# 64-bit weights of an attention and two feed-forward blocks: the conversion to 32 bits done in the loaded tile by a rescale, a shift, the sign and an integer addition

## The chip, the cores and the metric

The kernel runs on one core of a Trainium2 chip. The metric is the time of one execution on the device in microseconds (us). The core's engines run side by side and wait for one another by semaphores: TensorE (PE, with PEld for its weight loads), VectorE (DVE), ScalarE (ACT), GpSimd (POOL) and SyncE (SP), whose queue issues all the loads and stores here.

## What is computed

Three blocks follow one another. The attention block takes `x` (8 batches, 8 heads, 512 rows of 64) and `state` (8, 8, 32 rows of 64): the rows of x read the state by a softmax over 32, and the state reads x by a softmax over 512. Its output, 544 rows per batch, is 4352 rows of 512. Then come

```
h = maximum(x @ w_in, 0)            # w_in  512 x 2048
x = (h * h) @ w_out                 # w_out 2048 x 512
y = (((x @ w1) * (x @ w2)) @ w3) @ w_out2   # 512 x 1024 twice, 1024 x 1024, 1024 x 512
```

The inputs are arrays of 32-bit and 64-bit floats: x and state come as 32-bit, all six weight matrices as 64-bit floats. The output is 32-bit, 4352 x 512.

## The kernel before

**Matmuls in three passes.** An operand is split into a high part, rounded to the matmul's own 32-bit type, and a low part, the remainder (`split`, L80 to L85: the high part a copy, mostly on ScalarE, the low part a subtraction on VectorE). A product is three matmuls, high x high, low x high and high x low.

**First stage (up to about 640 us).** An outer loop goes over tiles (c, f), c a batch (or 8, for the state's rows of all batches), f one of 16 blocks of 128 columns of `w_in`. `h_tile` (L448) makes the hidden block, which ScalarE relus and squares and ScalarE and VectorE split (`ghl`); `y_tile` (L483), two tiles behind, multiplies it by the row block f of `w_out` into four accumulators (L494). `make_sw` (L421, matmuls at L426) makes state x `w_in` for a batch and 512 columns. For the first batches the attention steps (`att_steps`) run between the tiles. The first tiles need the converted blocks of `w_in` and `w_out` soon: `win0` in two halves of columns, each of two tiles, before and beside the first tiles; then `w_out` 0 to 7 and so on.

**Conversions.** All weights arrive as 64-bit words. One conversion handles 128 x 512 words: `load64` (L112) loads them into a raw tile of 128 x 512 x 2 32-bit words, low word first, so that the low and the high words are each every second word of the tile. `exponents` (L126) cuts the exponent bits out of the high words on VectorE (L128) and rescales them to the 32-bit exponent on ScalarE (L129, a relu with a bias tile). `convert64` (L132) then runs four operations on VectorE: the mantissa's upper bits as an integer (L146), plus the low words scaled by 2^-32 (L149), the sign bit into the exponent (L152), and mantissa times exponent into the target (L155). There are 72: four for `win0`, 12 for the rest of `w_in` and 16 for `w_out`, and 40 for the weights of the second block (`later`), which are stored to scratch in memory as 32-bit. A converted `w_out` block goes through the tile `cw` and is split (`make_wout`, L186).

**What sets the order.** `convs` (L568) lists the conversions; `conv` (L581) runs the next one, makes the exponents of the one after it ahead, and issues the load three further (`load_next`). Jobs hang on the tiles of the first stage by `side` and `late`, one `conv` per tile at first, from tile 32 on one for every second tile. Raw tiles come from a pool of three buffers (tag `raw`, L110), which loads of x share; the first few raw tiles lie in buffers of `w_out`. The exponents have two buffers (tag `ce`), the mantissa one (`cm`). The order written out is not the order on the engines: a planner orders each engine's instructions by its own estimate of when they can start, and gives the waits; `issue_after` ties a job to an instruction on its engine. On the chip each engine then works through its list in order.

**Later stages.** From about 640 us the second block's weights, all converted by then, are read back, multiplied together (L707) and used in `quad` (L822), `ab9` (L877) and `out_tile` (L903). Nothing of the change runs there but through the time at which it starts.

Of the kernel before, what the change touches and what calls it, by code (L numbers as in the profile page):

```python
# [8 lines left out]
F32 = mybir.dt.float32  # L9
F32R = mybir.dt.float32r  # L10
I32 = mybir.dt.int32
U32 = mybir.dt.uint32
ACTF = mybir.ActivationFunctionType
ALU = mybir.AluOpType
# [6 lines left out]
def kernel(  # L21
# [17 lines left out]
    nc = tc.nc  # L39
# [6 lines left out]
    P = 128  # L46
# [8 lines left out]
    scale = 1.0 / float(D) ** 0.5  # L55
# [3 lines left out]
    def f32(ap):  # L59
        return ap.bitcast(F32)  # L60

    const = ctx.enter_context(tc.tile_pool(name="const", bufs=1))
# [3 lines left out]

    ident = const.tile([P, P], F32, name="ident")
    make_identity(nc, ident)
    ebias = const.tile([P, 1], F32, name="ebias")
    nc.vector.memset(ebias, -896.0 * 2.0**23)  # L70
    def bank_m(name):
        return psum.tile([P, 512], F32, tag="m", bufs=2, name=name)

# [26 lines left out]
    att = att_cm.__enter__()  # L100
# [3 lines left out]
    raws = {}  # L104
# [16 lines left out]
            nc.sync.dma_start(flat, src.bitcast(I32))  # L121
        raws[key] = t

    exps = {}

    def exponents(key, t):  # L126
        e = att.tile([P, 512], I32, tag="ce", bufs=2, name="ce")
        nc.vector.tensor_single_scalar(e, t[:, :, 1], 0x7FF00000, op=ALU.bitwise_and)  # L128
        nc.scalar.activation(e, e, ACTF.Relu, bias=ebias, scale=8.0)  # L129
        exps[key] = e  # L130

    def convert64(key, out):  # L132


        t = raws.pop(key)
        hw, lw = t[:, :, 1], t[:, :, 0].bitcast(U32)
        if len(out.shape) == 3:
            n = out.shape[2]
            hw, lw = (v.rearrange("p (k n) -> p k n", n=n) for v in (hw, lw))
        if key not in exps:  # L140
            exponents(key, t)
        e = exps.pop(key)
        m = att.tile([P, 512], I32, tag="cm", bufs=1, name="cm")
        if len(out.shape) == 3:
            e, m = (v.rearrange("p (k n) -> p k n", n=n) for v in (e, m))
        nc.vector.tensor_scalar(  # L146
            out=m, in0=hw, scalar1=0xFFFFF, scalar2=0x100000, op0=ALU.bitwise_and, op1=ALU.bitwise_or
        )
        nc.vector.scalar_tensor_tensor(  # L149
            out=f32(m), in0=lw, scalar=2.0**-32, in1=m, op0=ALU.mult, op1=ALU.add  # L150
        )
        nc.vector.scalar_tensor_tensor(  # L152
            out=e, in0=hw, scalar=-(2**31), in1=e, op0=ALU.bitwise_and, op1=ALU.bitwise_or
        )
        nc.vector.scalar_tensor_tensor(  # L155
            out=out, in0=f32(m), scalar=2.0**-20, in1=f32(e), op0=ALU.mult, op1=ALU.mult
        )

    def load_win(fg, k):
        load64(("win", fg, k), w_in[k * P:(k + 1) * P, fg * 512:(fg + 1) * 512])  # L160
# [1 line left out]
    def make_win(fg, k):  # L162
        if k == 0:
            win_t[fg] = wpool.tile([P, ND, 512], F32, tag=f"wi{fg // 2}", bufs=2, name=f"win{fg}")
        convert64(("win", fg, k), win_t[fg][:, k, :])
# [6 lines left out]
    def make_win0(half, kk):  # L172
        if win_t[0] is None:
            win_t[0] = wpool.tile([P, ND, 512], F32, tag="wi0", bufs=2, name="win0")
        convert64(("win0", half, kk), win_t[0][:, 2 * kk:2 * kk + 2, half * 256:(half + 1) * 256])
# [6 lines left out]
    def close_splits():  # L182
        while open_splits:
            open_splits.pop(0)()

    def make_wout(f):  # L186
        w = att.tile([P, 512], F32, tag="cw", bufs=1, name="cw")
        convert64(("wo", f), w)

        def halves():  # L190
            t = wpool.tile([P, 2, DM], F32R, tag="wo", bufs=NF, name=f"wo{f}")
            split(t[:, HI], t[:, LO], w)
            wo_t[f] = t

        open_splits.append(halves)
# [330 lines left out]
        nc.scalar.copy(stT[:, 4 * half:4 * half + 4].rearrange("p b k n -> p (b k n)"), ps)  # L526

    warm = const.tile([P, 1], F32, name="warm")
    nc.scalar.activation(warm, ebias, ACTF.Exp, scale=0.0)
    for g in range(G):  # L530
        load_x(0, g, True)
    load_win0(0, 0, True)
# [42 lines left out]
    def load_next():  # L575
        k = convs[pos[0]] if pos[0] < len(convs) else None
        pos[0] += 1
        if k:
            {"wo": load_wout, "win": load_win, "later": load_later}[k[0]](*k[1:])

    def conv():  # L581


        close_splits()
        k, k1 = (convs[i] if i < len(convs) else None for i in (pos[1], pos[1] + 1))
        pos[1] += 1
        if k and k not in exps:
            exponents(k, raws[k])
        if k1:
            exponents(k1, raws[k1])  # L590
        if k:
            {"wo": make_wout, "win": make_win, "later": make_later}[k[0]](*k[1:])
            load_next()
# [6 lines left out]
    side[0] = [lambda: make_win0(1, 0), lambda: make_win0(1, 1), s2[0]]  # L600
    side[1] = [*xp1, lambda: make_sw(0, 0, slice(256, 512)), lambda: make_wout(0), a2t[0], s2[1], sc1]
    side[2] = [conv, s1a1[0], a2t[1], s1b1[0], at1[0]]
    side[3] = [conv, s21[0], sr, s1a1[1], srt, a2t1[0], conv, s1b1[1], sw(1, 0), at1[1]]
    side[4] = [conv, s21[1], lambda: make_st(1)]
    side[5] = [conv, a2t1[1]]
    side[6] = [conv, conv, sr1]
# [401 lines left out]
```

## Time and profile before

| what | value |
| --- | --- |
| time, median of 3 runs | 1257.79 us (1257.4 to 1259.08) |
| profiled execution | 1257.84 us, its span 1256.1 us |
| TensorE busy | 1235.1 us, 98% of the span |
| VectorE busy | 789.0 us, 63% |
| ScalarE busy | 659.3 us, 52% |
| TensorE's granted clock, mean | 0.999 |

The span goes from the first instruction to the last. Busy times of the engines overlap. The profile is of one execution; a line of it names the line of the code, the engine, the operation, and the tiles written and read. TensorE's granted clock is the share of full speed: 1.0 is 2.4 GHz, and a stretch with a value between 0.5 and 1.0 had a part at 1.2 GHz.

### The profile page before, as it was taken

The numbers are of one execution on the slowest core, as the hardware profiler recorded it, in microseconds if no ns is written. First come the engines' busy times: TensorE is split into PE (matmuls) and PEld (weight loads), VectorE is DVE, ScalarE is ACT, GpSimd is POOL, SyncE is SP. The second block draws the span as 40 slices with busy tenths as digits, with TensorE's granted clock in tenths as the row PEclk, the third lists the DMA queues.
The fourth block names the chain that finished last, engine by engine and source line by source line (L and its number), as shares of the span: only waits on it lengthen the run. The fifth ranks groups of instructions, "written<-read, shape, count | busy, mean of one in ns | idle before, by whom it ended". The sixth has DMA issues, their size and how long they took to land.

```text
span 1256.1 us, 17499 instructions
## 1 busy us (share of the span) xinstructions
PE 1235.1 (98%) x6672; PEld 982.1 (78%) x6672; DVE 789.0 (63%) x1403; ACT 659.3 (52%) x1188; POOL 33.5 (3%) x30
## 2 busy tenths in 40 slices
PE   6999999999999999999999999999999999999998
PEld 4667777777777777777799888888888888887886
DVE  6998778677585867742435835555655647474753
ACT  5687768666575756645655434444443524242430
POOL 0000000000000000000000000001500010000000
PEclk9999999999999999999999999999999999999999
DMA  6264646462634535201313520313430521423213
GB/s 218 69 207 145 173 129 201 113 184 82 156 130 86 190 76 173 89 18 34 134 42 111 201 76 9 120 48 126 143 134 9 201 76 52 149 74 128 76 59 117
DMA packets 125268, 143.23 MB, mean 114 GB/s; under 512 B 71680, under 2 KB 75264, under 8 KB 124672
## 3 DMA queue, kind: packets, MB, share of 16 engines
q1 hardware_dynamic: 125184, 142.11, 36.5%
q8 instruction: 52, 0.85, 0.3%
q14 instruction: 32, 0.26, 0.1%
HBM read 96.47 MB, written 45.61 MB: 113 GB/s over the span
## 4 chain that ended last, share of the span: by engine, by line
PE 93%; DMA 2%; ACT 2%; DVE 2%; issue 1%; SPq 0%; ACTq 0%; DVEq 0%
PE y L494 29%; PE po L903 14%; PE qa L822 10%; PE qd L822 7%; PE qc L822 3%; PE ps_w L707 3%; PE qe L822 3%; PE ps_sw L426 3%; PE ab L877 2%; DMA x<-in_x_dram 1%; PE ps_w L692 1%; PE ps_a L364 1%; PE ps_r L372 0%; PE ps_s L295 0%; DMA out_dram<-o 0%
## 5 line engine op out<-in xcount | busy, mean ns | idle before, releaser
L494 PE MATMUL y<-ghl,wo 128*128 128x512 f32 (+1 forms) x1728 | 403.0, 381 | 0.6 <-ACT wo L84 0.5
L494 PEld LDWEIGHTS y<-ghl,wo 128*128 128x128 f32 x1728 | 309.1, 188 | 88.4 <-ACT r L442 12.6
L85 DVE TENSOR_TENSOR ghl<-r,ghl 128x512 fp32r<-128x512 f32 (+1 forms) x144 | 95.0, 660 | 170.1 <-ACT ghl L84 167.4
L822 PE MATMUL qa<-yq,wq 128*128 128x512 f32 x576 | 146.3, 390 | 1.4 <-ACT s L830 1.4
L830 ACT COPY s<-qa 128x512 f32<-128x512 f32 x96 | 56.2, 589 | 143.7 <-PE qa L822 131.2
L822 PEld LDWEIGHTS qa<-yq,wq 128*128 128x128 f32 x576 | 107.5, 188 | 25.5 <-ACT s L830 2.4
L822 PE MATMUL qd<-yq,wq 128*128 128x512 f32 x384 | 98.4, 390 | 0.0
L903 PE MATMUL po<-w34b,c 128*128 128x512 f32 x408 | 95.8, 391 | 0.3 <-DVE o L912 0.3
L903 PE MATMUL po<-w,c 128*128 128x512 f32 x408 | 95.5, 391 | 0.0
L903 PEld LDWEIGHTS po<-w34b,c 128*128 128x128 f32 x408 | 75.7, 188 | 18.0 <-DVE c L85 1.0
L903 PEld LDWEIGHTS po<-w,c 128*128 128x128 f32 x408 | 75.5, 188 | 17.7 <-ACT o L909 1.1
L444 ACT ACTIVATE r<-r 128x512 f32<-128x512 f32 (+1 forms) x144 | 87.5, 608 | 2.9
L84 ACT CAST ghl<-r 128x512 fp32r<-128x512 f32 (+1 forms) x144 | 86.0, 597 | 3.5
L822 PEld LDWEIGHTS qd<-yq,wq 128*128 128x128 f32 x384 | 71.8, 188 | 15.7 <-ACT s L830 0.9
L129 ACT ACTIVATE ce<-ce,ebias 128x512 int32<-128x512 int32 x72 | 52.3, 727 | 44.3 <-DVE ce L128 44.3
L834 DVE TENSOR_TENSOR s<-qa,s 128x512 f32<-128x512 f32 x32 | 22.1, 692 | 75.0 <-ACT s L830 75.0
L780 POOL TENSOR_TENSOR yraw<-yraw,yp 128x512 f32<-128x512 f32 x24 | 32.8, 1373 | 987.9 <-DMA yraw<-yscr 815.2
L84 ACT CAST c<-s 128x512 fp32r<-128x512 f32 x64 | 39.7, 622 | 37.1 <-DVE s L851 36.1
L84 ACT CAST yq<-yraw 128x512 fp32r<-128x512 f32 x70 | 42.6, 622 | 24.1 <-DVE yraw L797 15.5
L912 DVE TENSOR_TENSOR o<-po,opart 128x512 f32<-128x512 f32 x34 | 23.3, 689 | 47.1 <-PE po L903 37.6
L152 DVE SCALAR_TENSOR_TENSOR ce<-raw,ce 128x512 int32<-128x512 int32 x72 | 49.3, 685 | 1.7 <-ACT ce L129 1.7
L85 DVE TENSOR_TENSOR yq<-yraw,yq 128x512 fp32r<-128x512 f32 x70 | 46.8, 684 | 5.0 <-ACT yq L84 4.7
(551 smaller groups left out, 1806.6 us busy)
## 6 DMA issues: line engine op xcount, KB each, us to landing
raw<-in_moe_w_dram SPq DMA_DIRECT2D x32, 512.0 KB, 4.3
yraw<-yscr SPq DMA_DIRECT2D x56, 256.0 KB, 5.5
yscr<-yo SPq DMA_DIRECT2D x52, 256.0 KB, 2.6
raw<-in_moe_w_out_dram SPq DMA_DIRECT2D x24, 512.0 KB, 3.9
oscr<-o SPq DMA_DIRECT2D x34, 256.0 KB, 2.2
opart<-oscr SPq DMA_DIRECT2D x34, 256.0 KB, 2.9
out_dram<-o SPq DMA_DIRECT2D x32, 256.0 KB, 2.9
raw<-in_moe_w_in_dram SPq DMA_DIRECT2D x12, 512.0 KB, 3.9
```

The source lines that it names most:

```text
L84: nc.scalar.copy(hi, src)
L85: return nc.vector.tensor_tensor(out=lo, in0=src, in1=f32(hi), op=ALU.subtract)
L129: nc.scalar.activation(e, e, ACTF.Relu, bias=ebias, scale=8.0)
L152: nc.vector.scalar_tensor_tensor(out=e, in0=hw, scalar=-(2**31), in1=e, op0=ALU.bitwise_and, op1=ALU.bitwise_or)
L426: mm = nc.tensor.matmul(pss[r][k * NS:(k + 1) * NS, cols], stT[rows, b, k, :], win_t[fg][rows, k, cols], start=True, stop=True, tile_posit ...
L444: nc.scalar.activation(r[:, :n], r[:, :n], ACTF.Square)
L494: nc.tensor.matmul(y_ps[c, d][:, :n], wo_t[f][:, wi, d * P:(d + 1) * P], t[:, gi, :n], start=(f == f0 and k == 0), stop=(f == f1 - 1 and k ...
L707: nc.tensor.matmul(ps, t[:, wi, (j % 4) * P:(j % 4 + 1) * P], wo2_t[j][:, vi, :], start=(j == 0 and k == 0), stop=(j == N1 - 1 and k == 2),)
L780: nc.gpsimd.tensor_tensor(out=t[:, n], in0=t[:, n], in1=p, op=ALU.add)
L822: nc.tensor.matmul(ps, W[w, kt][:, wi, m * P:(m + 1) * P], Y[v, kt][:, vi, :], start=(first and kt == 0 and k == 0), stop=(last and kt == ...
L830: nc.scalar.copy(t, ps)
L903: nc.tensor.matmul(ps, v[:, vi, t * P:(t + 1) * P], w[:, wi, :], start=(m == 0 and k == 0), stop=(m == QM - 1 and k == 2),)
```

## The change

The exponents go, and with them the mantissa tile and the bias tile. The high word, read as a 32-bit float, is multiplied by 2^-112 and written over the low word of the same weight in the raw tile, then shifted left by three bits in place; that rebiases the exponent and puts the upper mantissa bits in place. The sign bit of the high word is put in. ScalarE has before that scaled the low words by 2^-29 into an integer of at most 8, in a tile of its own (tag `ce`, now three buffers). An integer addition of the two gives the 32-bit pattern of the weight, rounded, in the target. `low_words` takes the place of `exponents` in `conv`, one conversion ahead as before. The warm-up activation reads a tile of zeros.

```diff
-    ebias = const.tile([P, 1], F32, name="ebias")
-    nc.vector.memset(ebias, -896.0 * 2.0**23)
+    zero = const.tile([P, 1], F32, name="zero")
+    nc.vector.memset(zero, 0.0)
...
-    exps = {}
-
-    def exponents(key, t):
-        e = att.tile([P, 512], I32, tag="ce", bufs=2, name="ce")
-        nc.vector.tensor_single_scalar(e, t[:, :, 1], 0x7FF00000, op=ALU.bitwise_and)
-        nc.scalar.activation(e, e, ACTF.Relu, bias=ebias, scale=8.0)
-        exps[key] = e
+    lows = {}
+
+    def low_words(key, t):
+        r = att.tile([P, 512], I32, tag="ce", bufs=3, name="ce")
+        nc.scalar.activation(r, t[:, :, 0].bitcast(U32), ACTF.Copy, scale=2.0**-29)
+        lows[key] = r
 
     def convert64(key, out):
         t = raws.pop(key)
-        hw, lw = t[:, :, 1], t[:, :, 0].bitcast(U32)
+        hw = t[:, :, 1]
+        if key not in lows:
+            low_words(key, t)
+        r = lows.pop(key)
+        m = t[:, :, 0]
+        nc.vector.tensor_single_scalar(f32(m), f32(hw), 2.0**-112, op=ALU.mult)
+        nc.vector.tensor_single_scalar(m, m, 3, op=ALU.logical_shift_left)
+        nc.vector.scalar_tensor_tensor(
+            out=m, in0=hw, scalar=-(2**31), in1=m, op0=ALU.bitwise_and, op1=ALU.bitwise_or
+        )
         if len(out.shape) == 3:
...
-        nc.vector.tensor_scalar(
-            out=m, in0=hw, scalar1=0xFFFFF, scalar2=0x100000, op0=ALU.bitwise_and, op1=ALU.bitwise_or
-        )
-        nc.vector.scalar_tensor_tensor(
-            out=f32(m), in0=lw, scalar=2.0**-32, in1=m, op0=ALU.mult, op1=ALU.add
-        )
-        nc.vector.scalar_tensor_tensor(
-            out=e, in0=hw, scalar=-(2**31), in1=e, op0=ALU.bitwise_and, op1=ALU.bitwise_or
-        )
-        nc.vector.scalar_tensor_tensor(
-            out=out, in0=f32(m), scalar=2.0**-20, in1=f32(e), op0=ALU.mult, op1=ALU.mult
-        )
+            m, r = (v.rearrange("p (k n) -> p k n", n=out.shape[2]) for v in (m, r))
+        nc.vector.tensor_tensor(out=out.bitcast(I32), in0=m, in1=r, op=ALU.add)
...
-        if k and k not in exps:
-            exponents(k, raws[k])
+        if k and k not in lows:
+            low_words(k, raws[k])
         if k1:
-            exponents(k1, raws[k1])
+            low_words(k1, raws[k1])
```

## Rows read from the trace of the kernel before

**Rows 1.** The page, first part: busy us (share of the span) xinstructions.

```profile
PE 1235.1 (98%) x6672; PEld 982.1 (78%) x6672; DVE 789.0 (63%) x1403; ACT 659.3 (52%) x1188; POOL 33.5 (3%) x30
```

**Rows 2.** Windows: stretch and length, busy us of each engine, clock, DMA.

```profile
24.60:31.90 7.30, 3.48 (x24) 1.99 (x22) 7.30 (x18) 6.66 (x13) 0.00 (x0) 1.00 0.46 175
30.00:40.00 10.00, 8.35 (x50) 4.39 (x49) 8.17 (x22) 6.95 (x15) 0.00 (x0) 0.83 0.00 1
31.90:100.00 68.10, 64.22 (x461) 43.39 (x462) 60.87 (x130) 52.33 (x99) 0.00 (x0) 0.97 0.42 140
100.00:600.00 500.00, 499.91 (x2913) 380.79 (x2912) 336.49 (x636) 317.12 (x552) 0.00 (x0) 1.00 0.43 123
```

**Rows 3.** Chain of waits from 24 us on: start us, us on the chain, what.

```profile
24.61 0.42 DVE ce L128
25.03 0.34 DVE cm L146
...
26.90 0.60 DVE nm L306
...
28.70 0.60 DVE ghl L85
...
29.64 0.06 DVE nm L308
...
31.24 0.61 DVE win L155
...
31.89 1.13 PE ps_sw L426 x8
```

**Rows 4.** VectorE's groups by shape: tiles, shapes, count | busy us, mean ns | idle before.

```profile
L85 DVE TENSOR_TENSOR ghl<-r,ghl 128x512 fp32r<-128x512 f32 x128 | 88.2, 689 | 163.5 <-ACT ghl L84 161.5 <-PE ps_a L350 2.0
L152 DVE SCALAR_TENSOR_TENSOR ce<-raw,ce 128x512 int32<-128x512 int32 x72 | 49.3, 685 | 1.7 <-ACT ce L129 1.7
L149 DVE SCALAR_TENSOR_TENSOR cm<-raw,cm 128x512 f32<-128x512 uint32 x72 | 49.2, 683 | 0.4
...
L128 DVE TENSOR_SCALAR ce<-raw 128x512 int32<-128x512 int32 x72 | 30.2, 420 | 4.7 <-DMA raw<-in_moe_w_in_dram 2.3 <-DMA raw<-in_moe_w_out_dram 1.8 <-DVE rs L313 0.3
...
L155 DVE SCALAR_TENSOR_TENSOR win<-cm,ce 128x512 f32<-128x512 f32 x16 | 11.0, 689 | 0.4
...
L85 DVE TENSOR_TENSOR ghl<-r,ghl 128x256 fp32r<-128x256 f32 x16 | 6.8, 424 | 6.6 <-ACT ghl L84 5.9
```

**Rows 5.** ScalarE's groups by shape, the same columns.

```profile
L444 ACT ACTIVATE r<-r 128x512 f32<-128x512 f32 x128 | 80.8, 631 | 2.8
...
L129 ACT ACTIVATE ce<-ce,ebias 128x512 int32<-128x512 int32 x72 | 52.3, 727 | 44.3 <-DVE ce L128 44.3
...
L444 ACT ACTIVATE r<-r 128x256 f32<-128x256 f32 x16 | 6.7, 420 | 0.1
```

**Rows 6.** Chain of waits, 0 to 100 us, pieces behind 32 us.

```profile
37.32 0.61 ACT ce L129
...
47.30 0.60 DVE ce L152
...
47.93 3.98 DMA x<-in_x_dram
...
66.69 4.43 DMA raw<-in_moe_w_out_dram
```

**Rows 7.** Waits, 20 to 100 us: us in total, times, longest.

```profile
PE ps_sw L426 <- ACT xT L287: 3.7, 2, 2.6
...
DVE ce L128 <- DMA raw<-in_moe_w_out_dram: 1.1, 1, 1.1
```

**Rows 8.** Waits of SyncE's queue, 20 to 120 us.

```profile
SPq L121 <- DVE cm L149: 28.3, 7, 13.8
```

**Rows 9.** Timeline of ScalarE at 25 us: start, us, what [idle before it, releaser].

```profile
25.06 0.73 ACT L129 ACTIVATE ce<-ce,ebias 128x512 int32<-128x512 int32 x1 [1.09 <-DVE ce L128]
```

**Rows 10.** VectorE's groups, 24.6 to 100 us.

```profile
L149 DVE SCALAR_TENSOR_TENSOR cm<-raw,cm 128x512 f32<-128x512 uint32 x14 | 9.5, 679 | 0.1
```

More of the change, by code (lines that the diff above doesn't have):

```diff
@@ L122, in load64 @@
         raws[key] = t
-    exps = {}
-    def exponents(key, t):
-        e = att.tile([P, 512], I32, tag="ce", bufs=2, name="ce")
-        nc.vector.tensor_single_scalar(e, t[:, :, 1], 0x7FF00000, op=ALU.bitwise_and)
-        nc.scalar.activation(e, e, ACTF.Relu, bias=ebias, scale=8.0)
-        exps[key] = e
+    lows = {}
[3 more added lines that the diff above has]
+        lows[key] = r
     def convert64(key, out):
         t = raws.pop(key)
-        hw, lw = t[:, :, 1], t[:, :, 0].bitcast(U32)
-        if len(out.shape) == 3:
[L138 to L145, printed above, removed]
-        nc.vector.tensor_scalar(
-            out=m, in0=hw, scalar1=0xFFFFF, scalar2=0x100000, op0=ALU.bitwise_and, op1=ALU.bitwise_or
-        )
-        nc.vector.scalar_tensor_tensor(
-            out=f32(m), in0=lw, scalar=2.0**-32, in1=m, op0=ALU.mult, op1=ALU.add
-        )
-        nc.vector.scalar_tensor_tensor(
-            out=e, in0=hw, scalar=-(2**31), in1=e, op0=ALU.bitwise_and, op1=ALU.bitwise_or
-        )
-        nc.vector.scalar_tensor_tensor(
-            out=out, in0=f32(m), scalar=2.0**-20, in1=f32(e), op0=ALU.mult, op1=ALU.mult
-        )
+        hw = t[:, :, 1]
[8 more added lines that the diff above has]
+        )
+        if len(out.shape) == 3:
+            m, r = (v.rearrange("p (k n) -> p k n", n=out.shape[2]) for v in (m, r))
+        nc.vector.tensor_tensor(out=out.bitcast(I32), in0=m, in1=r, op=ALU.add)
     def load_win(fg, k):
@@ L528 @@
     warm = const.tile([P, 1], F32, name="warm")
-    nc.scalar.activation(warm, ebias, ACTF.Exp, scale=0.0)
+    nc.scalar.activation(warm, zero, ACTF.Exp, scale=0.0)
     for g in range(G):
```

## The prediction

> **What bounds the kernel now.** I read the busy shares first: TensorE is busy for 1235.1 of 1256.1 us [rows 1], so a change on VectorE and ScalarE can win at most TensorE's holes. The windows say where these are [rows 2]. From 100 to 600 us, where most conversions run, TensorE is busy for 499.91 of 500 us, with VectorE at 336 us and ScalarE at 317 us: there a conversion is hidden whatever it costs, as long as it adds less than some 160 us. From 24.6 to 31.9 us TensorE is busy for 3.48 of 7.30 us while VectorE is busy for all of it, and from 31.9 to 100 us it is busy for 64.22 of 68.10 us with VectorE at 60.87. The holes of these two windows are 3.82 + 3.88 = 7.7 us. The rest of TensorE's 21.0 us of holes lies in the first 24.6 us, where loads set the pace, or after 600 us, behind the last conversion; I leave it as it is. From 30 to 40 us the granted clock is 0.83, a mean of its two levels (1.2 and 2.4 GHz) after the idle stretch before it: 10 x 0.17 = 1.7 us of full-pace work lost [rows 2]. More than 9.4 us is thus not to be had.
>
> Then the chain of waits [rows 3]. From 24.61 to 31.85 us it lies on VectorE without a break, and releases `ps_sw` (L426) at 31.89. It holds the conversions of the two halves of `win0` (rows for L128, L146, L149, L152, L155), the first operation of a third conversion, and a maximum (0.60), two splits of ghl (0.60 each) and a small one (0.06). In the chain an operation takes the step to the next: 0.34 us for one of 0.42, 0.60 us for one of 0.68. So 15 pieces make 0.42 + 4 x 0.34 + 9 x 0.60 + 0.06 = 7.24, against 31.85 - 24.61 = 7.24.
>
> **The change, part by part.**
>
> *VectorE.* Before, a conversion is five operations: two of one source (L128 0.42, L146 the same step in [rows 3]) and three of two sources (L149, L152, L155: 0.68 to 0.69) [rows 4]; in steps 2 x 0.34 + 3 x 0.60 = 2.48 us. After, it is four: the rescale and the shift (one source), the sign (two sources), the addition (two sources). L128 reads every second word and still takes 0.42 us, and L149 and L152, with one such source, cost what the L155 with none does. So reading the stepping column is free. Two things no row shows: writing a stepping column, which the first three now do, and an integer addition of 32-bit words.
> - Rescale and shift: 0.42 us (as L128 and L146), or 0.69 if the stepping write takes the second element per cycle away. Less is not to be had: L128 is the fastest row with this size.
> - Sign: 0.68 us (as L152), or, if the stepping write doubles the time per element, more. Two rows of one operation [rows 4] give (689 - 424) / 256 = 1.04 ns per element and 159 ns fixed; doubled that is 159 + 1060 ns = 1.22 us, in steps 1.14.
> - Addition: 0.69 us as the TENSOR_TENSOR of ghl of this size, or, if a word goes through as two halves, 1024 elements, 1.22 us by the same slope. I take 0.69, the row of the same instruction and size.
>
> The Trainium skill, "DVE: scalar operands, raw-bit mode, write accounting and state across instructions", section "Raw-bit mode", says that VectorE's fp32 addition is exact on raw patterns only while operands and sum stay below 2^24; by that an exact sum of 32-bit words must be built of pieces. That is the 1.22 us end, and the conversion would then gain nothing (first rival).
>
> With 0.69 a conversion takes 0.34 + 0.34 + 0.60 + 0.60 = 1.88 us in steps, 0.60 less. On the path from 24.61 to 31.85: two conversions 3.76, the others 0.60 + 1.20 + 0.06; L128 of the third conversion has gone to ScalarE. With 0.08 for the first one, which stands at 0.42, that is 5.70 instead of 7.24 us: **1.5 us** gained. The other condition of this point is `xT` from ScalarE, for which TensorE waited 3.7 us in two waits [rows 7]; it comes earlier too, since ScalarE sat idle 1.09 us at 25.06 waiting for L128 [rows 9] and no longer needs it.
>
> *ScalarE.* L129 takes 0.727 us, with a bias read from a tile; L444, an activation with none, 0.631 [rows 5]. The low words are scaled by constants alone, so 0.63 us, if the stepping source costs ScalarE nothing, as on VectorE. That no row shows; bounds 0.63 and, with 512 elements more at (631 - 420) / 256 = 0.82 ns by the L444 rows, 1.05. Three L129 steps stand on the chain between 37 and 93 us, the first in [rows 6]: 3 x 0.10 = **0.3 us**. The other 69 are beside TensorE. The third tile takes the room of `cm`. It lets the low words of the next conversion be made while two earlier ones are pending, so I cost the tile at nothing; the cover is ScalarE's lead of one conversion.
>
> *Order and waits.* The rescale now overwrites the low words, so it waits for ScalarE to have read them. For all but the first conversions that is done one conversion ahead. For the first, the load, ScalarE 0.63, then four operations replace L128, ScalarE 0.73, then two: within 0.3 us of each other, and the x loads set the end there. Queued behind a waiting rescale on VectorE are the splits of ghl, wo and sw, for which TensorE waits.
> The raw tile is freed by the addition now; before, mostly by L149, for which SyncE's queue waited 28.3 us in seven waits [rows 8]. One chain piece is such a load: L152 ends (47.30 + 0.60) and the load of x starts at 47.93 [rows 6]. There 0.34 + 0.34 + 0.60 + 0.60 stands for the old L128, L146, L149, L152 (1.88 too): nothing gained.
>
> *The rest of the stage.* Of the 14 conversions between 24.6 and 100 us [rows 10] 12 are left, 12 x 0.60 = 7.2 us less on a VectorE that is busy 60.87 of 68.10 us. Not all of it is on the path: after 53 us most chain pieces are TensorE, ScalarE or loads. TensorE's holes there are 3.88 us; I take a quarter, **1.0 us**. After 100 us nothing.
>
> Sum: 1.5 + 0.3 + 1.0 = 2.8 us. The profiled execution took 1257.84 us (span 1256.1 and 1.7 around it), within 0.1 us of the median of 1257.79: 1255.0 us.
>
> **Rivals.**
> 1. *The gain is eaten.* If the addition takes 1.22 us (1.14 in steps), a conversion is 2.42 against 2.48: on the first stretch 2 x 2.42 + 0.08 + 1.86 = 6.78, 0.5 us gained, and 0.3 on ScalarE: 1257.0 us. A second way to the same: the loads at 47.93 and 66.69 [rows 6] start one step of 0.60 later because the addition frees the tile, 2.8 - 1.2 = 1.6: 1256.2 us. A third: ScalarE, in order, now takes the wait for a load that VectorE took (1.1 us for w_out [rows 7]), with relu and the splits behind it: 1256.1 us. For it: the chain is made of such loads. Against: at 66.69 it is ScalarE's copy of x that frees the tile.
> 2. *Slower: the stepping column.* If writing it costs an element per two cycles, the rescale and the shift step at 0.60, sign 1.14, and an addition of halves 1.14: 3.48 us, 1.00 more than before. First stretch: 2 x 3.48 + 0.08 + 1.86 = 8.90, 1.7 us more. Then 12 us more in a stage where VectorE has 68.10 - 60.87 = 7.2 us free: at least 4.8 on the path. 1.7 + 4.8 - 0.3 = 6.2: 1264.0 us. It decides from 2.48 us per conversion, and in earnest from 2.48 + 7.2 / 12 = 3.08. For it: three operations write what none wrote before. Against: reading such a column is free in two kinds of operation.
> The Trainium skill, "Vector Engine (DVE) Microarchitecture Reference", section "Measured stream behaviour on trn2", says that a port keeps its rate only if elements come in runs of at least two neighbouring words, and gives 1.73 ns for a source and 1.71 for a destination that hops at every element. L149 and L152 differ from it: sources that step by two words take 0.683 to 0.685 us, where it would give an estimated 1.04. For the destination no row speaks; by the page the sign would take about 1.03 us.
> 3. *More than forecast.* The planner orders the instructions anew; if all of TensorE's holes of the stage close and the clock stays up: 1.5 + 0.3 + 3.9 + 1.7 = 7.4: 1250.4 us.
>
> **How the numbers follow.** What can be told from no change here is 0.2%, 2.5 us: faster is below 1255.3, slower above 1260.3. Forecast, with the third case as its far end: 0.50, its own range 1250.4 to 1256.5. Of it 0.43 lies below 1255.3, as the quarter that I took may well be a half. First rival 0.30, of which 0.02 below 1255.3. Second rival 0.20, of which 0.17 above 1260.3. The range 1250.5 to 1261.0 leaves out the far end of the forecast and most of the second rival. Faster 0.45, same 0.38, slower 0.17.
>
> **What would show it.** Right: no activation waits for VectorE; four operations per conversion of 0.42, 0.42, 0.68 and 0.69; `ps_sw` near 30.4 instead of 31.89; the holes before 100 us at about 5 us; 100 to 600 us as before. The first rival shows as an addition near 1.2 us, or as loads that end the chain's waits more than before. The second shows as a sign operation above 1 us and VectorE full up to 100 us. The forecast is wrong if the holes before 100 us stay above 7 us, or if a new one opens behind 100 us.

## The result and the profile after

The changed kernel took 1267.61 us (median of 6 runs, 1261.8 to 1268.42), the kernel before 1257.94 us in 6 runs beside it: a ratio of 1.0065, 95% interval 1.0054 to 1.0077. It is slower by 8.2 us by the ratio (6.8 to 9.7), by 9.7 between the medians. The forecast was 1255.0 us, in a range of 1250.5 to 1261.0: wrong in sign, and outside the range. The profiled execution is the one of 1268.42 us, with a span of 1266.6 us, 10.5 us more than the span before.

The page's first part, columns as in [rows 1], changed kernel:

```profile
PE 1239.2 (98%) x6672; PEld 985.1 (78%) x6672; DVE 746.7 (59%) x1331; ACT 656.2 (52%) x1188; POOL 33.9 (3%) x30
```

VectorE works 42 us less than in [rows 1], as meant. TensorE has 1266.6 - 1239.2 = 27.4 us of holes instead of 21.0, and its matmuls take 4.1 us longer in sum: 6.4 + 4.1 = 10.5. The windows tell where, columns as in [rows 2]:

```profile
0.00:24.60 24.60, 15.57 (x117) 11.82 (x118) 14.10 (x30) 14.34 (x25) 0.70 (x6) 1.00 0.80 237
24.60:31.90 7.30, 5.37 (x31) 2.86 (x30) 6.83 (x15) 5.22 (x10) 0.00 (x0) 0.87 0.34 139
30.00:40.00 10.00, 10.00 (x46) 5.94 (x46) 6.78 (x20) 6.81 (x15) 0.00 (x0) 0.66 0.00 1
31.90:100.00 68.10, 66.49 (x464) 45.64 (x461) 54.70 (x119) 53.99 (x102) 0.00 (x0) 0.96 0.44 140
100.00:600.00 500.00, 491.61 (x2862) 373.61 (x2861) 301.00 (x573) 306.99 (x540) 0.00 (x0) 0.99 0.43 123
600.00:1266.60 666.60, 660.17 (x3207) 551.20 (x3205) 370.06 (x596) 275.71 (x512) 33.23 (x24) 1.00 0.29 98
```

| stretch | holes before, us | holes after, us |
| --- | --- | --- |
| to 24.6 | 7.74 | 9.03 |
| 24.6 to 100 | 7.70 | 3.54 |
| 100 to 600 | 0.09 | 8.39 |
| from 600 | 5.52 | 6.43 |

In holes, the stage that the change aimed at gained 4.2 us and the stretch that was full lost 8.3 (before 24.6 and from 600 us, TensorE was busy for 16.86 and 650.58 us before), with fewer operations on VectorE (301.00 us against 336.49) and on ScalarE (306.99 against 317.12) than it had. The same matmul can be followed through both traces: at 99 us the changed kernel is 2.3 us ahead, at 297 us 0.2 behind, at 385 us 2.0, at 450 us 5.9, at 539 us 9.3, and from there to the end the distance grows by only 1.2. (All such positions are of the profiled executions.)

The operations cost what was forecast. VectorE's groups by shape, columns as in [rows 4], and ScalarE's one group of the change, as [rows 5]:

```profile
L140 DVE SCALAR_TENSOR_TENSOR raw<-raw 128x512 int32<-128x512 int32 x72 | 49.5, 688 | 1.5
...
L145 DVE CUSTOM_DVE_ANT_0 cw<-raw,ce 128x1024 uint16<-128x1024 uint16 x56 | 38.1, 680 | 1.3 <-DMA w12s<-cw 0.6 <-DMA w3s<-cw 0.3
L138 DVE TENSOR_SCALAR raw<-raw 128x512 f32<-128x512 f32 x72 | 30.1, 421 | 9.5 <-ACT ce L128 7.8 <-DMA st<-in_state_dram 1.7
L139 DVE TENSOR_SCALAR raw<-raw 128x512 int32<-128x512 int32 x72 | 30.0, 419 | 0.8
```

```profile
L128 ACT ACTIVATE ce<-raw 128x512 int32<-128x512 uint32 x72 | 48.6, 677 | 39.4 <-DMA raw<-in_moe_w_in_dram 15.9 <-DMA raw<-in_moe_w_dram 11.8 <-DMA raw<-in_moe_w_out_dram 10.4
```

The last row also holds what went wrong: ahead of the 72 activations ScalarE stood idle for 39.4 us, nearly all of it waiting for a load to land. In [rows 5] ScalarE's step (L129) had 44.3 us of idle time ahead of it, but waiting for VectorE. The waits of the changed kernel from 100 to 600 us (us in total, times, longest):

```profile
ACT ce L128 <- DMA raw<-in_moe_w_dram: 11.8, 15, 1.5
...
ACT ce L128 <- DMA raw<-in_moe_w_out_dram: 9.0, 6, 3.6
...
PE ps_a L352 <- DVE sw L85: 7.5, 5, 2.5
...
ACT ce L128 <- DMA raw<-in_moe_w_in_dram: 6.6, 3, 2.3
```

ScalarE waits 24 times for a load here, 27.4 us in all. Before, it was VectorE that could wait for one, and it did so for 0.6 us in the whole stretch. And 7.5 of TensorE's 8.4 us of holes are five waits of `ps_a` (L352), a transpose of the softmax's result that the attention steps of each of the middle batches issue, for VectorE's half of the split of `sw`.

The chain of waits shows how the two hang together. Changed kernel, around the hole at 444 us (start, us on the chain, what):

```profile
434.63 4.17 DMA raw<-in_moe_w_dram
...
438.82 0.67 ACT ce L128
439.50 0.48 ACT r L430
439.98 0.51 ACT aT L84
...
441.05 0.63 ACT ghl L84
...
442.31 0.68 DVE cw L145
442.99 0.61 DVE mx L317
...
446.21 0.61 DVE sw L85
...
446.86 1.12 PE ps_a L352 x4
447.98 2.30 PE ph__4475 L444 x6
...
453.04 1.36 PE ph__4519 L444 x6
```

The load lands at 438.80 us. Only then does ScalarE, in order, make the low words, and only then the relu, the splits of aT and of ghl behind them. VectorE's list has the addition of a conversion ahead of the softmax's maximum (`mx`), the exponential waits for that, and the split of `sw` for the exponential. The timelines at that place, changed kernel first (start, us, what, idle before and its releaser):

```profile
438.82 0.67 ACT L128 ACTIVATE ce<-raw 128x512 int32<-128x512 uint32 x1 [1.19 <-DMA raw<-in_moe_w_dram]
...
444.35 0.63 ACT L323 ACTIVATE e<-e 128x512 f32<-128x512 f32 x1 [1.52 <-DVE e L318]
444.88 0.60 ACT L84 CAST ghl<-r 128x512 fp32r<-128x512 f32 x1
...
446.86 1.12 PE L352 MATMUL ps_a<-ident,e 128*128 128x128 f32 x4 [2.53 <-DVE sw L85]
```

and the kernel before, same batch:

```profile
439.70 0.62 ACT L84 CAST ghl<-r 128x512 fp32r<-128x512 f32 x1
...
440.48 0.63 ACT L335 ACTIVATE e<-e 128x512 f32<-128x512 f32 x1 [0.16 <-DVE e L330]
...
441.64 1.28 DVE L85 TENSOR_TENSOR sw<-ps_sw,sw 128x512 fp32r<-128x512 f32 x2
...
442.38 0.66 PE L364 MATMUL ps_a<-ident,e 128*128 128x128 f32 x4
```

Before, ScalarE stood idle for 0.16 us ahead of the exponential and TensorE did not wait; after, for 1.52 us, and TensorE stood for 2.53 us. The chain into `ps_a` goes back to a load's landing in four of the five waits (at 220, 370, 447 and 524 us); at 294 us, a wait of 0.57 us, it holds no load. Windows of the changed kernel give what the hole costs behind it:

```profile
446.80:449.90 3.10, 3.04 (x10) 2.58 (x11) 3.10 (x9) 1.28 (x2) 0.00 (x0) 0.51 0.00 0
449.90:455.00 5.10, 5.10 (x24) 4.20 (x23) 1.52 (x3) 2.42 (x4) 0.00 (x0) 1.00 0.47 157
...
525.00:528.50 3.50, 3.50 (x10) 2.76 (x9) 3.09 (x8) 1.81 (x4) 0.00 (x0) 0.52 0.04 16
```

For the 3.1 us behind it the granted clock is 0.51, the lower of the two levels, 1.2 GHz; the chain has six matmuls of `ph` at 2.30 us there and at 1.36 once the clock is back. A second such stretch stands behind the wait at 524 us (1.85 us, clock 0.52); behind the other three, of 0.57 to 1.82 us, the clock stayed at 1.00. By these two windows the clock cost an estimated 3.2 us of full-pace work, and with the 8.3 us of holes that makes 11.5 of the 11.6 us that the matmul followed above lost between 99 and 539 us. The clock before 100 us adds to the 4.1 us of longer matmuls (0.95 from 24.6 to 100 us, 0.98 before). The one run of 1261.8 us had a mean clock of 0.999, the other five 0.994 to 0.995, which fits. Both kernels' splits of `sw` have the same work; what differs is the order in which ScalarE and VectorE come to it.

### The profile page after: what moved, and what is told of

Its sections match the earlier page's. It is cut to its first block, busy times and chain, and to the rows that moved or that the text cites. A ratio compares the mean times of both kernels' runs of the same rounds, so it can differ in the third digit from the quotient of the medians.

```text
span 1266.6 us, 17443 instructions
## 1 busy us (share of the span) xinstructions
PE 1239.2 (98%) x6672; PEld 985.1 (78%) x6672; DVE 746.7 (59%) x1331; ACT 656.2 (52%) x1188; POOL 33.9 (3%) x30
## 4 chain that ended last, share of the span: by engine, by line
PE 78%; DMA 8%; DVE 7%; ACT 5%; issue 2%; SPq 1%; DVEq 0%; ACTq 0%
PE y L482 21%; PE po L891 12%; PE qa L810 10%; PE qd L810 7%; PE qc L810 3%; PE ps_w L695 3%; PE qe L810 3%; DMA raw<-in_moe_w_dram 2%; PE ab L865 2%; PE ps_sw L414 2%; DMA raw<-in_moe_w_in_dram 1%; ACT ghl L84 1%; DVE cw L145 1%; DMA raw<-in_moe_w_out_dram 1%; ACT r L432 1%
## 5 line engine op out<-in xcount | busy, mean ns | idle before, releaser
L128 ACT ACTIVATE ce<-raw 128x512 int32<-128x512 uint32 x72 | 48.6, 677 | 39.4 <-DMA raw<-in_moe_w_in_dram 15.9
L140 DVE SCALAR_TENSOR_TENSOR raw<-raw 128x512 int32<-128x512 int32 x72 | 49.5, 688 | 1.5
L810 PE MATMUL qc<-yq,wq 128*128 128x512 f32 x192 | 49.5, 391 | 0.0
```

Of the source, the lines that this page charges most:

```text
L128: nc.scalar.activation(r, t[:, :, 0].bitcast(U32), ACTF.Copy, scale=2.0**-29)
L140: nc.vector.scalar_tensor_tensor(out=m, in0=hw, scalar=-(2**31), in1=m, op0=ALU.bitwise_and, op1=ALU.bitwise_or)
L810: nc.tensor.matmul(ps, W[w, kt][:, wi, m * P:(m + 1) * P], Y[v, kt][:, vi, :], start=(first and kt == 0 and k == 0), stop=(last and kt == ...
```

## The experiments

The theory (T). In the kernel before, the first operation of the lookahead (L128) ran on VectorE. The job `conv` is listed under `issue_after(done[i - 3])`, and `done` holds VectorE's splits of ghl. The tie binds instructions of VectorE alone, and so held the whole conversion back, ScalarE's step too, since that needs L128's result. The change put the first operation on ScalarE, where nothing ties it, and with three tiles no wait for a free tile holds it either. The planner then lists the low words as early as it believes the load landed (its belief is in no trace; the order that it gave is); ScalarE, in order, waits for the real landing with relu and splits behind it.

The rivals: the lookahead's place in the program is wrong (L, runs e1 and e2); the rescale written over the raw tile ties loads and engines together, and the mantissa should have kept its tile (F, run e3); the third tile alone does it (run e4).

| run | edit, against the changed kernel unless said | us | ratio to before, interval | TensorE busy 100 to 600 |
| --- | --- | --- | --- | --- |
| (after) | | 1267.61 | 1.0065, 1.0054 to 1.0077 | 491.61 |
| e1 | low words written a tile later | 1269.4 | 1.0083, 1.0066 to 1.0100 | 489.22 |
| e2 | no lookahead | 1266.93 | 1.0070, 1.0054 to 1.0085 | 490.17 |
| e3 | mantissa tile back, two low-word tiles | 1263.69 | 1.0044, 1.0029 to 1.0059 | 494.72 |
| e4 | two low-word tiles | 1259.54 | 1.0010, 1.0000 to 1.0019 | 496.29 |
| e5 | three tiles, tied four splits back | 1257.88 | 0.9988, 0.9979 to 0.9998 | 495.98 |
| e6 | tied three back | 1256.19 | 0.9980, 0.9970 to 0.9989 | 497.69 |
| e7 | e5 with two tiles | 1258.2 | 0.9997, 0.9987 to 1.0006 | 496.44 |
| e8 | kernel before, lookahead untied | 1264.37 | 1.0044, 1.0029 to 1.0059 | 495.84 |
| e9 | tied two back | 1259.0 | 1.0004, 0.9995 to 1.0013 | 496.28 |
| e10 | tied one back | 1255.72 | 0.9976, 0.9965 to 0.9987 | 499.40 |

### e1: the lookahead one tile later

```diff
+    def ahead():
+        k1 = convs[pos[1]] if pos[1] < len(convs) else None
+        if k1 and k1 not in lows:
+            low_words(k1, raws[k1])
...
-        if k1:
+        if k1 and now:
             low_words(k1, raws[k1])
...
+    for i in range(32, NF * B, 2):
+        side[i].append(lambda: conv(False))
+        side[i + 1].append(ahead)
```

> From the 32nd tile on, the low words of the next conversion are made one tile (about 4 us) after the conversion instead of with it; nothing else differs from the changed kernel (1267.6 us). Theory W (ScalarE, in order, stands at the low words of a tile whose load has not landed, and relu, splits and softmax behind it come late): ScalarE's waits for landings between 100 and 600 us fall from 27 us to under 8, TensorE's holes there from 8.4 us to under 3, time 1255 to 1259 us. Theory O (the planner's new order of the lists is bad in itself, whatever waits in it): holes stay at 6 to 10 us, time 1262 to 1270 us. Theory F (the addition frees the raw tile late, so loads start late): loads start as before, but their lateness is covered by the extra tile; as W.

Nothing was gained (1269.4 us). Waits, 100 to 600 us, as above:

```profile
ACT ce L128 <- DMA raw<-in_moe_w_dram: 14.4, 13, 1.8
...
PE ps_a L352 <- DVE sw L85: 9.5, 5, 2.8
...
ACT ce L128 <- DMA raw<-in_moe_w_out_dram: 9.1, 6, 4.3
```

The waits are close to those of the changed kernel (29.4 us for loads against 27.4). To see the order itself I counted, for each conversion, how many relus (L430 here, L442 before) ScalarE had issued ahead of that conversion's activation. In e1 the count equals the changed kernel's in all 72 conversions. The place in the program had no say in ScalarE's list, and so this run does not tell W, O and F apart.

### e2: no lookahead

```diff
-        if k1:
-            low_words(k1, raws[k1])
```

> The low words of a conversion are made with that conversion, none ahead. Theory W: ScalarE's waits for landings fall under 8 us from 27, since loads have one more conversion to land; in exchange VectorE's rescale waits for ScalarE in many of the 72 conversions, 0.7 us each, some of it in front of the splits; time 1256 to 1261 us. Theory O: 1262 to 1270 us. Theory F: as W, for the load has the same lateness and more time.

The same once more: 1266.93 us, 27.9 us of waits for loads, `ps_a` waiting 8.8 us in five waits, and the same counts but for one conversion. L fell with both: what the lookahead is written to do is not what orders the engines, and the planner pulls the low words ahead by itself.

### e3: the mantissa tile back

```diff
-        r = att.tile([P, 512], I32, tag="ce", bufs=3, name="ce")
+        r = att.tile([P, 512], I32, tag="ce", bufs=2, name="ce")
...
-        m = t[:, :, 0]
+        m = att.tile([P, 512], I32, tag="cm", bufs=1, name="cm")
```

> Rescale, shift and sign write a tile of their own (one buffer) instead of the loaded tile; two tiles instead of three for the scaled low words, for room. The raw tile is free after the sign operation, one or two VectorE operations before the addition. Theory F: loads start 0.6 to 1.5 us earlier, ScalarE's waits for landings fall from 27 us to under 12, holes between 100 and 600 us under 4 us, time 1255 to 1260 us. Theory W alone: waits shrink by at most 0.6 us for each of the 24, to 13 or more; holes 4 to 8 us; 1260 to 1266 us. Theory O: no tie to either, 1262 to 1270 us.

```profile
ACT ce L128 <- DVE cw L145: 23.6, 15, 2.2
...
PE ps_a L352 <- DVE sw L85: 3.4, 5, 0.7
```

These are its waits from 100 to 600 us. Of the waits for loads 1.0 us is left, since the low words now wait for a free tile instead. It takes 1263.69 us, and the holes are still 5.3 us: F expected under 4. e4 shows which of the two edits that is.

### e4: two tiles alone

```diff
-        r = att.tile([P, 512], I32, tag="ce", bufs=3, name="ce")
+        r = att.tile([P, 512], I32, tag="ce", bufs=2, name="ce")
```

> Two tiles instead of three for the scaled low words, nothing else. If the third tile is what lets ScalarE run ahead to a load that has not landed, waits and holes fall and the time is 1256 to 1261 us. By W and F in their plain form (the lookahead is one conversion either way, the addition frees the raw tile either way) nothing changes: ScalarE waits 20 to 30 us for landings, 1262 to 1269 us. By O the order changes a little and the time with it, either way by up to 5 us.

1259.54 us: with the rescale still in the raw tile, 4 us better than e3 on the same chip. F fell: freeing the raw tile earlier wins nothing. Followed by their matmuls, e3 goes from 0.9 us ahead of the kernel before at 100 us to 4.6 behind at 600, e4 from 4.1 ahead to 1.5 behind, so both lose the same there; what the mantissa tile costs in these two traces lies before 100 us, where e3's clock from 24.6 us on is 0.91 and e4's 0.98. And the third tile, which the prediction had cost at nothing, costs some 7 us in this kernel (ratios 1.0065 and 1.0010; 8.1 us between the medians). Two tiles hold the low words back by a wait:

```profile
ACT ce L128 <- DVE cw L145: 9.7, 9, 1.5
...
ACT ce L128 <- DMA raw<-in_moe_w_in_dram: 3.6, 3, 2.3
...
ACT ce L128 <- DMA raw<-in_moe_w_out_dram: 2.2, 2, 1.9
```

The waits for loads fall from 27.4 to 5.8 us, in place of them 9.7 us for the tile, as the first of the expectations had it. That is a brake, not yet an order: 3.7 us of holes are left.

### e5, e6, e7: the tie given back, on ScalarE

```diff
-            nc.scalar.copy(hi, src)
+            highs.append(nc.scalar.copy(hi, src))
...
-        nc.scalar.activation(r, t[:, :, 0].bitcast(U32), ACTF.Copy, scale=2.0**-29)
+        with tc.issue_after(acts[-4].ins) if len(acts) > 8 else nullcontext():
+            nc.scalar.activation(r, t[:, :, 0].bitcast(U32), ACTF.Copy, scale=2.0**-29)
...
         done.append(split(t[:, HI, :n], t[:, LO, :n], r[:, :n]))
+        acts.append(highs[-1])
```

This ties the low words to ScalarE's own split of ghl, as far back as the old tie was (e5); e6 has `acts[-3]`, e7 is e5 with `bufs=2`.

> The changed kernel with the low words' activation queued on ScalarE behind the high split of ghl three tiles back (issue_after, from the ninth tile on); three tiles as in the change. In the kernel before, the same job was queued behind the split three tiles back on VectorE, through L128; the change moved its first operation to ScalarE, where that tie does not hold. Theory T (the lost tie lets the planner put the low words where it thinks the load has landed, and ScalarE then waits for it with relu and splits behind): waits for landings between 100 and 600 us fall from 27 us to under 8, TensorE's holes there from 8.4 to under 3 us, the 2 to 4 us won before 100 us stay: 1254 to 1259 us. Rival P (three tiles as such, or the place of VectorE's four operations, make the planner's order worse at the batch's softmax): holes stay at 5 us or more, 1261 to 1268 us.

> As e5, queued one tile later (behind the split two tiles back). Theory T: ScalarE's waits for landings go down to under 4 us; the time is that of e5 within 2 us, or a little above if VectorE's rescale now waits for ScalarE (up to 40 times 0.7 us, mostly beside TensorE). Rival P: no better than e5.

> As e5 with two tiles for the scaled low words. Theory T: with the tie in place the number of tiles hardly matters: within 2 us of e5. Without the tie two tiles gave 1259.5 us and three 1267.6 us, so if the tile as such cost 8 us (rival P), it is 4 us or more below e5.

e5 takes 1257.88 us with the three tiles, about 10 us less than the changed kernel (ratios 0.9988 and 1.0065), and e6 1256.19. Waits for loads in e5 are 6.2 us, as T expected (under 8), but its holes from 100 to 600 us are 4.0 us: T expected under 3 and P 5 or more, so on the holes both missed. With the tie the number of tiles no longer matters (e5 and e7 lie 0.3 us apart), while without it the third tile costs some 7. So the tile is harmful only through the order that it allows. Waits and window of e6 from 100 to 600 us, whose lines are shifted (L133 the low words, L143 the rescale, L357 `ps_a`):

```profile
DVE raw L143 <- ACT ce L133: 7.2, 6, 1.4
...
PE ps_a L357 <- DVE sw L87: 2.3, 3, 0.8
```

```profile
100.00:600.00 500.00, 497.69 (x2899) 378.40 (x2898) 303.10 (x573) 311.26 (x546) 0.00 (x0) 1.00 0.44 123
```

Of the waits for loads 1.2 us is left in it (T: under 4), in two waits for blocks of `w_out`; VectorE waits for the low words instead. TensorE's holes of 100 to 600 us are 2.3 us instead of 8.4, and the clock is at 1.00.

### e8: the kernel before, with its tie taken away

```diff
-        if k1:
+        if k1 and k1 not in exps:
             exponents(k1, raws[k1])
...
+        if i >= 8:
+            for job in side.get(i, ()):
+                if job is conv:
+                    for k in convs[pos[1]:pos[1] + 2]:
+                        if k not in exps:
+                            exponents(k, raws[k])
         gate = done[i - 3] if i >= 8 else first if i == 0 else None
         with tc.issue_after(gate.ins) if gate else nullcontext():
```

The exponents of the next two conversions are listed ahead of the tied block; the old arithmetic stays as it was.

> The kernel before with the exponents of the next two conversions of a tile traced ahead of the block that queues the tile's jobs, so that L128 is no longer queued behind the split three tiles back; all else as before. Theory T, from its other side: L128 moves up on VectorE to where the planner thinks the load has landed, VectorE waits for landings (0.6 us between 100 and 600 us before) by 5 us or more, and the time rises by 1 to 6 us over 1258.5; the two exponent tiles hold it back more than three would. Rival P: within 1 us of 1258.5.

It takes 1264.37 us, 5.6 more than the kernel before beside it (1258.76). VectorE's and TensorE's waits, 100 to 600 us:

```profile
PE ps_a L364 <- DVE sw L85: 2.8, 4, 0.8
DVE ce L128 <- DMA raw<-in_moe_w_dram: 2.8, 3, 1.0
...
DVE ce L128 <- DMA raw<-in_moe_w_out_dram: 1.3, 2, 1.0
```

With 0.7 us for `w_in` VectorE waits 4.8 us for loads, against 0.6 with the tie (T expected 5 or more): the waits of T, and TensorE's wait at `ps_a`, in a kernel that has nothing of the change but the loss of the tie. The loss lies where T puts it: by its matmuls e8 is 0.2 us behind the kernel before at 100 us and 4.5 at 600, with 4.2 us of holes between. The waits for loads are fewer than ScalarE's 27.4, so this run shows the sign of the tie's worth rather than the changed kernel's 10 us.

### e9, e10: the tie moved closer

The edit is that of e5 with `acts[-2]` and `acts[-1]`.

> As e6 (1256.2 us), queued one tile later still: behind the high split one tile back. By theory T the waits for landings are gone already with e6, so no more is to be had there: 1254 to 1258 us. If the order of VectorE's list is the rest of it (its rescale now stands later, away from the splits of a batch's softmax), the holes between 100 and 600 us fall from 2.3 to about 1 us and the time to 1254 to 1256 us. Against it: VectorE waits more for ScalarE (7.2 us with e6).

> Queued behind the high split of the tile just traced. Theory T: ScalarE never waits for a landing; the low words come so late that the rescale of the next conversion waits for them, with splits of ghl and sw behind it on VectorE: VectorE waits 10 us or more for ScalarE, the holes between 100 and 600 us rise over 3 us, 1256 to 1262 us; the best place lies between e5 and e10.

Both expectations missed, in opposite directions: e9 takes 1259.0 us, e10 1255.72, the lowest median (not clear of e6 by the ratios) and 0.24% (0.13 to 0.35) below the kernel before. The window of e10 from 100 to 600 us, and ScalarE's timeline at the place of the hole, e10 first, then e9:

```profile
100.00:600.00 500.00, 499.40 (x2909) 380.37 (x2908) 307.73 (x575) 314.92 (x549) 0.00 (x0) 1.00 0.44 123
```

```profile
435.55 0.67 ACT L133 ACTIVATE ce<-raw 128x512 int32<-128x512 uint32 x1
436.13 0.61 ACT L328 ACTIVATE e<-e 128x512 f32<-128x512 f32 x1
...
438.21 0.62 ACT L86 CAST ghl<-r 128x512 fp32r<-128x512 f32 x1
438.74 1.07 ACT L86 CAST sw<-ps_sw 128x512 fp32r<-128x512 f32 x2
```

```profile
438.27 0.63 ACT L328 ACTIVATE e<-e 128x512 f32<-128x512 f32 x1 [0.93 <-DVE e L323]
438.81 0.60 ACT L86 CAST ghl<-r 128x512 fp32r<-128x512 f32 x1
```

TensorE of e10 is busy for 499.40 of the 500 us; the low words start without a wait, the split of `sw` stands 3.2 us after them, and `ps_a` does not wait. VectorE, for which 10 us or more of waits for ScalarE were expected, does not wait for the low words here. The order, as relus ahead of the activation of conversions 41 to 48:

| kernel | relus ahead |
| --- | --- |
| before | 47 48 49 51 52 54 56 58 |
| after, e1 and e2 | 48 49 50 50 52 53 54 56 |
| e4 | 48 49 50 51 52 53 55 57 |
| e5 | 48 49 50 50 52 54 56 58 |
| e6 | 48 49 50 51 53 55 57 59 |
| e9 | 48 49 50 52 54 56 58 60 |
| e10 | 49 49 51 53 55 57 59 61 |

The changed kernel makes the last low words of the row two relus earlier than the kernel before; e10 makes them three later. But e5's row ends as that of the kernel before does, with 4.0 us of holes against 0.09, and e9 is later than e6 and 2.8 us slower: how late the low words stand is not the whole of it. In e9 `ps_a` waits 2.6 us in four waits and no load is waited for. The lists at the softmax show what does it. In the last three batches of the stretch (`ps_a` at about 366, 441 and 516 us in e9) the chain into `ps_a` runs in e5, e6 and e9 through VectorE's rescale, shift, sign and addition of one conversion, which stand among the softmax's transposes and ahead of its maximum; the exponential comes late, and ScalarE's copy of `ghl`, though its input is ready, is listed behind it, with the split of `sw` behind that. The kernel before lists that copy ahead of the exponential (439.70 us above), and e10 has the four operations behind the maximum and the exponential 2 us before the copy is due; neither waits. The changed kernel (444.35 and 444.88 us above) has the order of e9, and a load's landing ahead of it. Why the planner picks one order or the other, I cannot say by rule.

## Why the prediction was wrong

- **The operations: right.** 0.421, 0.419, 0.688 and 0.680 to 0.689 us against 0.42, 0.42, 0.68 and 0.69. The stepping write is free, so the second rival falls, and with it the condition that it set at 3.08 us a conversion. The Trainium skill ("Vector Engine (DVE) Microarchitecture Reference", section "Measured stream behaviour on trn2") speaks against that write: it has a port at full rate only for runs of two neighbouring words, and 1.71 ns for a destination that hops 4 KiB at every element, by which the sign would take an estimated 1.03 us. This trace has 0.688 for a step of two words, so the measurement decides. The addition shows in halves, as the first rival supposed (1024 halves of 16 bits), but takes the time of 512 words. ScalarE's step took 0.677 us: inside the bounds of 0.63 and 1.05, near the value taken.
- **The first stretch and the stage to 100 us: right in size.** The forecast was 2.8 us by 100 us; at 99 us the changed kernel is 2.3 ahead. The holes are 3.5 us where about 5 were forecast. What was not foreseen is the clock: 0.66 from 30 to 40 us instead of 0.83, and holes in the first 24.6 us of 9.03 instead of 7.74. The first `ps_sw` does not start near 30.4 but at 29.41 us.
- **"After 100 us nothing": the step that failed.** It rested on a sum: TensorE full for 499.91 of 500 us and VectorE and ScalarE with some 160 us to spare each. Slack in sum says that the work fits, not that each engine comes to it in time. ScalarE's list was reordered, and 27.4 us of waits and 8.3 us of holes came into a stretch with less work on both engines. The clock behind two of the holes cost some 3 us more.
- **"I cost the tile at nothing; the cover is ScalarE's lead of one conversion": the same error from the other side.** That lead was to be had at any number of tiles, as e5 and e7 show. What the third tile added was freedom to be early, and that cost some 7 us (e4).
- **The rival that came nearest was priced wrong.** The first rival's third way named the mechanism: "ScalarE, in order, now takes the wait for a load that VectorE took", with the relu and the splits behind it. I priced it by one wait of 1.1 us from 20 to 100 us [rows 7]. It occurred 24 times after 100 us. The reason why VectorE had so few such waits there, the tie to `done`, stood in the code: the operation that the tie held was the one that moved to another engine. The second way, loads that start late because the addition frees the tile, was not what cost the time: e3 frees the tile earlier and wins nothing.

What the change is worth when the full stretch stays full is shown by e10: 3.0 us below the kernel before beside it (1258.68 to 1255.72), against the forecast of 2.8. By its matmuls it is 2.9 us ahead at 100 us and 2.0 at 600, so the gain lies where the forecast had it. That the sizes agree so closely is in part luck: other orders of the same operations are 5.2 us ahead at 100 us (e6) and 5.5 (e9).

Shown: the tie and the third tile together decide (after, e4, e5, e7), the lookahead's place in the program, where no tie holds it, does not (e1, e2), the arithmetic is not at fault (e8 loses 5.6 us without it, e10 wins with it). Only in part settled is how much of the loss is the wait for a load and how much the mere order. In the last three batches `ps_a` waits 1.82, 2.53 and 1.85 us in the changed kernel and 0.78, 0.77 and 0.76 in e9, which has the same order there and no wait for a load; by this an estimated 3.9 of 6.2 us are the load's. e3, with 1.0 us of waits for loads and still 5.3 us of holes, fits that order alone costs. Earlier loads with the order kept, which would settle it, were not tried. Also open: in e9 1.8 us of what it lost on the kernel before lie after 600 us, where nothing of the change runs.

## What to carry to other kernels

When a change moves an operation to another engine, look for everything that held the old one in its place (a tie to an instruction, a tile to wait for, an operand from a slower engine) and ask whether it holds on the new engine. In this kernel an operation that starts from a fresh load did better tied to its own engine's work than left to the planner (1255.7 to 1259.0 us against 1267.6); a spare buffer let it move up, and was no gift there. Where it stands among its neighbours counts besides how late it stands. A full TensorE is no proof of a margin: ask of each of its waits which chain releases it, and what the change puts into that chain.

## What the runs showed of the hardware

- An integer addition of 32-bit words appears as an operation on 1024 halves of 16 bits and takes 0.680 to 0.689 us, as much as a subtraction of 512 32-bit floats (0.689 in [rows 4]).
- Writing every second 32-bit word of a tile costs VectorE nothing: 0.421 us where L128 in [rows 4] wrote without steps in 0.420.
- ScalarE's activation that reads every second word takes 0.677 us, against 0.631 for one without steps and bias [rows 5].
- A hole of 2.53 us in TensorE's work was followed by about 3 us at a granted clock of 0.51, and one of 1.85 us by a stretch at 0.52, so these two `ps_a` waits cost more than their length. Behind the other three waits, of 0.57 to 1.82 us, the clock stayed at 1.00, and in e1 so it did from 371.27 to 375 us behind a wait of 2.74 us: by these rows the length of the hole alone does not decide.
